# The last three of 96 feed-forward steps cut into halves of 256 columns, where before only the last one was

## The chip, the cores and the metric

The kernel runs on one core of a Trainium2 chip. The metric is the device time of one execution in microseconds (us), as the median of several. Five engines work at once, each through its own queue in the order of that queue: PE (matmuls), ACT (ScalarE), DVE (VectorE), POOL (GpSimd) and SP, which only issues DMAs here. Where one engine needs what another makes, the program has semaphore waits.

## The reference

```python
# attention part: a gated recurrence over 768 time steps, for 4 batches x 8 heads of width 40
attn_out = _attn_ref(q, k, v, i_gate, f_gate, o_gate)
x = attn_out.transpose(0, 2, 1, 3).reshape(3072, 320)
# feed-forward part
h = x @ w_in                                  # (3072, 2048)
h2 = h * h
h3 = h2 * h
P = a[0] + a[1] * h + a[2] * h2 + a[3] * h3
Q = 1.0 + np.abs(b[0]) * np.abs(h) + np.abs(b[1]) * h2
g = P / (Q + 1e-06)
return (g @ w_out).astype(np.float32)         # (3072, 320)
```

The change is in the feed-forward part alone.

## The kernel before, in words

The 3072 tokens go through the feed-forward part in 12 blocks of 256, and each block in 8 steps of 256 of the 2048 hidden features. One step, `feed_forward(n, i)` (line 1098), works on a tile of 128 partitions by 512 columns (`W`, line 1101): columns 0 to 255 (`T` = 256) are the 256 tokens for one group of 128 features, columns 256 to 511 the same tokens for the next group. So the two halves of a step need nothing of each other until their products are added up in `po`. The attention part runs ahead of the feed-forward blocks that need it; in the last block, number 11, no attention work is left.

What one step does, with the names of the planner's operations, the engine, and how a row of the trace shows it:

- `f1` on PE: h = x @ w_in into `ph`, 16 matmuls, 8 for each half. `ph` has one PSUM tile of 128x512 for the whole step (`f_f1`, line 1109), out of a pool of four (`psH`, line 422).
- `ha` (`ha<-ph`), `u` (`w<-ha,ba`) and `p1` (`p<-ph,ps`) on ACT: |h|, a linear form of it, and a shifted square of h.
- `p3` on DVE (`p<-p,ps,ph`): the cubic's next product.
- `w` on POOL (`w<-w,ha`): the denominator Q but for its constant.
- `y` (`ph<-w,cd`) and `r0` (`ph<-ph`) on ACT: 1/Q, by a reciprocal square root and a square, written over h in `ph`.
- `gH` on DVE (`gH<-p,ps,ph`): g in the rounded form that PE takes. Then `m` on DVE (`w<-w,gH`), `rm` on POOL (`p<-p,w`) and `gL` on DVE (`gL<-p,ps,ph`) make the remainder that the rounding left.
- `f2` and `f3` on PE: gH times w_out (8 matmuls) and gL times w_out (4) are added up in `po`, over all 8 steps of a block.
- `ev`: after a block's last step `po` goes to SBUF, in the last block on ACT for its first 128 tokens and on DVE for the others (`ot<-po`), and from there to DRAM by DMA.

A step is written for either form: `cuts` (line 1101) is one slice of 512 columns, or two of 256, and `each` (line 1213) records an operation once for each cut.

```python
last = NS * n + i >= NS * NU // 2 - HALVED                                     # line 1100
cuts = [slice(j * T, (j + 1) * T) for j in range(2)] if last else [slice(0, W)]  # line 1101
...
plan.add(
    f"{name}{'half' if last and part is not None else ''}_{k}", base + FFN_AT[name] + at, engine, cost, fn,
...
for j, c in enumerate(cuts):
    add(
        name, engine, cost * 0.6 if last else cost, lambda c=c: fn(c), r, w,
```

What sets the order: `_Plan` (line 58) gathers all operations with a key and an estimated cost. `order` (line 96) simulates the engines with these costs and gives each engine its queue; of the operations that are about ready it takes the one with the smallest key. The key comes from the table `FFN_AT` (line 173) plus an entry of `NUDGE` (line 196) for this one operation of this one step, if there is one. An operation of a step in halves carries the word "half" in its name, and so has no entry in `NUDGE`. The semaphore waits are put in when the program is built, from the tiles that instructions read and write.

Below, y6.0 is operation y of step 6 of block 11, its first half; y6 is that operation undivided.

Of the kernel before, what the change touches and what calls it, by code (L numbers as in the profile page):

```python
# [190 lines left out]
FIRST = -40  # L191
EARLY = 3
HOT = 90
HALVED = 1

NUDGE = dict(
    raw_j0=20.54, s0_j0=4.61, o0_j0=47.59, raw_i0=-37.31, s0_i0=-2.65, o0_i0=-60.48, o2_i0=-57.94, raw_o0=-4.06,
# [178 lines left out]
def _program(  # L376
# [721 lines left out]
    def feed_forward(n, i):  # L1098
        d = {}
        last = NS * n + i >= NS * NU // 2 - HALVED  # L1100
        cuts = [slice(j * T, (j + 1) * T) for j in range(2)] if last else [slice(0, W)]
# [207 lines left out]
```

## Time and profile before

| | us |
|---|---|
| median of 3 runs | 570.61 (570.03 to 570.77) |
| time of the profiled execution | 571.71 |
| its span, from the first to the last instruction | 569.9 |
| PE busy | 527.2 (93%) |
| DVE busy | 476.2 (84%) |
| ACT busy | 430.9 (76%) |
| POOL busy | 394.5 (69%) |

The rows are of the one profiled execution, which took 1.1 us more than the median; 1.8 us of its time lie outside its span. Times in rows are from the span's start. A row of the order of time gives the start, the length, the engine, the operation with what it writes and reads, how many instructions stand in it, and in brackets the engine's idle time before it with what ended that.

### The profile page before, as it was taken

How to read it: one execution, taken by the hardware profiler on the slowest of the kernel's cores; microseconds unless marked ns; L12 is line 12 of the kernel's file. 1: busy time of each engine (PE TensorE's matmuls, PEld its weight loads, DVE VectorE, ACT ScalarE, POOL GpSimd, SP SyncE). 2: the span in 40 equal slices, each digit the busy share in tenths (PEclk: the TensorE clock that was granted, in tenths of full speed). 3: DMA queues.
4: the chain of work that ended last, by engine and by line, in shares of the span. 5: the costliest groups of instructions: out<-in, count | busy, mean ns of one | idle time of the engine just before them, and what ended most of it. 6: DMA issues, size and time to landing. Idle time of an engine off the chain costs nothing.

```text
span 569.9 us, 13096 instructions
## 1 busy us (share of the span) xinstructions
PE 527.2 (93%) x5024; PEld 493.6 (87%) x5024; DVE 476.2 (84%) x782; ACT 430.9 (76%) x757; POOL 394.5 (69%) x353
## 2 busy tenths in 40 slices
PE   4966896899999999999999999999999999999994
PEld 4964686799989999999999898899899999999993
DVE  8999888997888779988888877877987878878685
ACT  2567679776866888777788868888877777777982
POOL 4538469986677697777868684586777686757753
PEclk9877687999999999999999999999999999999998
DMA  5899966432331213332313214232122010000000
GB/s 171 183 258 243 224 170 139 85 69 56 88 66 55 60 45 81 62 72 78 79 35 85 36 50 97 64 66 74 33 62 73 15 36 2 1 26 1 23 1 30
DMA packets 120666, 44.10 MB, mean 77 GB/s; under 512 B 103826, under 2 KB 113106, under 8 KB 120594
## 3 DMA queue, kind: packets, MB, share of 16 engines
q1 hardware_dynamic: 120450, 43.01, 32.3%
q8 instruction: 41, 0.67, 0.5%
q14 instruction: 31, 0.25, 0.2%
q10 hardware_dynamic: 144, 0.16, 0.1%
HBM read 39.03 MB, written 4.13 MB: 76 GB/s over the span
## 4 chain that ended last, share of the span: by engine, by line
PE 69%; DVE 13%; POOL 5%; issue 4%; ACT 4%; DMA 2%; SPq 2%; DVEq 0%; POOLq 0%; ACTq 0%
PE ph L34 27%; PE po L34 25%; PE y L34 7%; PE ps L34 4%; PE kq L34 3%; PE ow L34 2%; DVE w L34 2%; DVE gH L34 2%; POOL p L34 2%; DVE gL L34 1%; ACT ph L34 1%; PE px L34 1%; DVE early_kT L34 1%; POOL w L34 1%; POOL tm L34 1%
## 5 line engine op out<-in xcount | busy, mean ns | idle before, releaser
L34 POOL TENSOR_TENSOR p<-p,w 128x512 f32<-128x512 f32 (+1 forms) x97 | 128.8, 1328 | 84.8 <-DVE w L34 78.1
L34 PE MATMUL ph<-xk,wi 128*128 128x256 f32 x1152 | 174.7, 287 | 0.9 <-DVE gL L34 0.7
L34 POOL TENSOR_TENSOR w<-w,ha 128x512 f32<-128x512 f32 (+1 forms) x97 | 138.5, 1428 | 36.4 <-ACT w L34 32.5
L34 PEld LDWEIGHTS ph<-xk,wi 128*128 128x128 f32 x1152 | 152.8, 189 | 6.0 <-issue 2.1
L34 PE MATMUL po<-wo,gH 128*128 128x320 f32 x768 | 135.8, 315 | 1.8 <-DVE gH L34 1.8
L34 PEld LDWEIGHTS po<-wo,gH 128*128 128x128 f32 x768 | 114.9, 188 | 4.8 <-DVE gH L34 2.6
L34 DVE SCALAR_TENSOR_TENSOR gH<-p,ps,ph 128x512 fp32r<-128x512 f32 (+1 forms) x97 | 71.6, 738 | 33.9 <-PE po L34 15.2
L34 ACT ACTIVATE ha<-ph 128x512 f32<-128x512 f32 (+1 forms) x97 | 57.4, 592 | 42.6 <-PE ph L34 42.3
L34 DVE SCALAR_TENSOR_TENSOR w<-w,gH 128x512 f32<-128x512 f32 (+1 forms) x97 | 84.3, 871 | 5.7 <-POOL p L34 0.5
L34 ACT ACTIVATE w<-ha,ba 128x512 f32<-128x512 f32 (+1 forms) x97 | 78.7, 811 | 4.8 <-POOL p L34 0.4
L34 ACT ACTIVATE ph<-w,cd 128x512 f32<-128x512 f32 (+1 forms) x97 | 66.2, 683 | 20.3 <-DVE p L34 14.4
L34 PE MATMUL po<-wo,gL 128*128 128x320 f32 x384 | 77.1, 318 | 4.3 <-DVE gL L34 4.1
L34 DVE SCALAR_TENSOR_TENSOR gL<-p,ps,ph 128x512 fp32r<-128x512 f32 (+1 forms) x97 | 71.2, 735 | 10.4 <-POOL p L34 8.8
L34 DVE SCALAR_TENSOR_TENSOR p<-p,ps,ph 128x512 f32<-128x512 f32 (+1 forms) x97 | 71.0, 736 | 4.3 <-ACT p L34 3.4
L34 PEld LDWEIGHTS po<-wo,gL 128*128 128x128 f32 x384 | 59.3, 188 | 8.4 <-DVE gL L34 6.6
L34 ACT ACTIVATE p<-ph,ps 128x512 f32<-128x512 f32 (+1 forms) x97 | 65.5, 675 | 0.9 <-DVE gL L34 0.7
L34 ACT ACTIVATE ph<-ph 128x512 f32<-128x512 f32 (+1 forms) x97 | 56.1, 579 | 2.7
L34 PE MATMUL ph<-xk,wj 128*128 128x256 f32 x192 | 54.3, 283 | 0.0
L34 PE MATMUL ph<-xk,wY 128*128 128x256 f32 x192 | 53.9, 281 | 0.0
L34 DVE TENSOR_TENSOR_SCAN e<-fb,eye 128x512 f32<-128x512 f32 x24 | 37.1, 1544 | 0.2
L34 PE MATMUL ps<-qb,kT 104*64 104x128 f32 x384 | 28.9, 297 | 8.2 <-ACT qb L34 5.5
L34 PEld LDWEIGHTS ph<-xk,wY 128*128 128x128 f32 x192 | 36.4, 190 | 0.0
(127 smaller groups left out, 788.7 us busy)
## 6 DMA issues: line engine op xcount, KB each, us to landing
fb<-scrF SPq DMA_DIRECT2D x48, 128.0 KB, 3.1
ab<-scrA SPq DMA_DIRECT2D x48, 128.0 KB, 3.3
rawo<-in_moe_w_out_dram SPq DMA_DIRECT2D x8, 640.0 KB, 5.9
rawi<-in_moe_w_in_dram SPq DMA_DIRECT2D x8, 512.0 KB, 5.6
og<-in_o_gate_dram SPq DMA_DIRECT2D x24, 160.0 KB, 3.4
kr<-in_k_dram SPq DMA_DIRECT2D x24, 160.0 KB, 2.8
qn<-in_q_dram SPq DMA_DIRECT2D x24, 160.0 KB, 3.4
vb<-in_v_dram SPq DMA_DIRECT2D x48, 80.0 KB, 2.8
```

Of the source, the lines that this page charges most:

```text
L34: made = fn(*args, **kwargs)
```

## The change

`HALVED` (line 194) goes from 1 to 3. So steps 5 and 6 of block 11 are cut as step 7 was already: for each of their eleven operations on ACT, DVE and POOL there are two of 128x256 in place of one of 128x512, 22 instructions more in all. PE has the same matmuls in the same order; half of `f2` and `f3` of these steps can now wait for half of gH and gL.

```diff
-HALVED = 1
+HALVED = 3
```

The names of these operations change, so they lose their entries in `NUDGE`, and their order with it. On ACT before, from step 6's first operation to step 7's (names: ha, w and p are the tiles of u, p1 and so on; the figure behind the name is the step):

```order
L34 ACTIVATE ha_6_7309<-ph_6_7279 128x512 [waits PE_49]
L34 ACTIVATE w_6_7318<-ha_6_7309,ba 128x512 [waits Activation_49,Pool_49]
L34 ACTIVATE p_6_7325<-ph_6_7279,ps 128x512 [waits DVE_49]
L34 ACTIVATE ph_5_7237<-w_5_7289,cd 128x512 [waits DVE_49,Pool_49]
L34 ACTIVATE ph_5_7237<-ph_5_7237 128x512 [waits Activation_49]
L34 ACTIVATE ph_6_7279<-w_6_7318,cd 128x512 [waits DVE_49,Pool_49]
L34 ACTIVATE ph_6_7279<-ph_6_7279 128x512 [waits Activation_49]
L34 ACTIVATE ha_7_7371<-ph_7_7327 128x256 [waits PE_49]
```

The same stretch of ACT after, up to y6.0:

```order
L34 ACTIVATE ha_6_7319<-ph_6_7279 128x256 [waits PE_49]
L34 ACTIVATE w_6_7324<-ha_6_7319,ba 128x256 [waits Activation_49,Pool_49]
L34 ACTIVATE ph_5_7237<-w_5_7288,cd 128x256 [waits DVE_49,Pool_49]
L34 ACTIVATE ph_5_7237<-ph_5_7237 128x256 [waits Activation_49]
L34 ACTIVATE ph_5_7237<-w_5_7288,cd 128x256 [waits Activation_49,Pool_49]
L34 ACTIVATE ph_5_7237<-ph_5_7237 128x256 [waits DVE_49]
L34 ACTIVATE p_6_7361<-ph_6_7279,ps 128x256
L34 ACTIVATE ha_6_7319<-ph_6_7279 128x256
L34 ACTIVATE w_6_7324<-ha_6_7319,ba 128x256 [waits Activation_49]
L34 ACTIVATE p_6_7361<-ph_6_7279,ps 128x256
L34 ACTIVATE ha_7_7385<-ph_7_7329 128x256 [waits PE_49]
L34 ACTIVATE ph_6_7279<-w_6_7324,cd 128x256 [waits DVE_49,Pool_49]
```

Step 6's p1.0, ha.1, u.1 and p1.1 stand behind step 5's y and r0 now, where p1 and all of ha and u stood ahead of them; and r05.1 has a wait on DVE. On DVE before, from p3 of step 6 to gH of step 7:

```order
L34 SCALAR_TENSOR_TENSOR p_6_7325<-p_6_7325,ps,ph_6_7279 128x512 [waits PE_49,Activation_49]
L34 SCALAR_TENSOR_TENSOR gH_5_7355<-p_5_7301,ps,ph_5_7237 128x512 [waits DVE_49,PE_49,Activation_49]
L34 SCALAR_TENSOR_TENSOR w_5_7289<-w_5_7289,gH_5_7355 128x512 [waits DVE_49]
L34 SCALAR_TENSOR_TENSOR gH_6_7373<-p_6_7325,ps,ph_6_7279 128x512 [waits PE_49,Activation_49]
L34 SCALAR_TENSOR_TENSOR w_6_7318<-w_6_7318,gH_6_7373 128x512 [waits DVE_49,Pool_49]
L34 SCALAR_TENSOR_TENSOR gL_5_7388<-p_5_7301,ps,ph_5_7237 128x512 [waits Pool_49]
L34 SCALAR_TENSOR_TENSOR p_7_7382<-p_7_7382,ps,ph_7_7327 128x256 [waits Activation_49]
L34 SCALAR_TENSOR_TENSOR p_7_7382<-p_7_7382,ps,ph_7_7327 128x256
L34 SCALAR_TENSOR_TENSOR gL_6_7405<-p_6_7325,ps,ph_6_7279 128x512 [waits PE_49,Pool_49]
L34 SCALAR_TENSOR_TENSOR gH_7_7411<-p_7_7382,ps,ph_7_7327 128x256 [waits DVE_49,PE_49,Activation_49]
```

The same stretch of DVE after:

```order
L34 SCALAR_TENSOR_TENSOR p_6_7361<-p_6_7361,ps,ph_6_7279 128x256 [waits Activation_49]
L34 SCALAR_TENSOR_TENSOR gL_5_7376<-p_5_7293,ps,ph_5_7237 128x256 [waits Pool_49]
L34 SCALAR_TENSOR_TENSOR p_6_7361<-p_6_7361,ps,ph_6_7279 128x256 [waits Activation_49]
L34 SCALAR_TENSOR_TENSOR gH_6_7401<-p_6_7361,ps,ph_6_7279 128x256 [waits DVE_49,PE_49,Activation_49]
L34 SCALAR_TENSOR_TENSOR w_6_7324<-w_6_7324,gH_6_7401 128x256 [waits DVE_49]
L34 SCALAR_TENSOR_TENSOR gH_6_7401<-p_6_7361,ps,ph_6_7279 128x256 [waits Activation_49]
L34 SCALAR_TENSOR_TENSOR w_6_7324<-w_6_7324,gH_6_7401 128x256 [waits DVE_49,Pool_49]
L34 SCALAR_TENSOR_TENSOR gL_6_7422<-p_6_7361,ps,ph_6_7279 128x256 [waits PE_49,Pool_49]
L34 SCALAR_TENSOR_TENSOR p_7_7413<-p_7_7413,ps,ph_7_7329 128x256 [waits Activation_49] x2
L34 SCALAR_TENSOR_TENSOR gL_6_7422<-p_6_7361,ps,ph_6_7279 128x256 [waits Pool_49]
L34 SCALAR_TENSOR_TENSOR gH_7_7435<-p_7_7413,ps,ph_7_7329 128x256 [waits PE_49,Activation_49]
```

Step 5's gH and m stand ahead of p3 of step 6 now, where p3 of step 6 stood ahead of them; and p3 of step 7 stands behind gH and m of both halves of step 6 and behind gL6.0, each half of it with a wait on ACT.

## Rows read from the trace of the kernel before

**Rows 1.** The page's chain that ended last: share of the span by engine.
```profile
PE 69%; DVE 13%; POOL 5%; issue 4%; ACT 4%; DMA 2%; SPq 2%; DVEq 0%; POOLq 0%; ACTq 0%
```

**Rows 2.** PE in order of time, the last 12 us.
```profile
558.23 0.86 PE L34 MATMUL po<-wo,gL 128*128 128x320 f32 x4 [1.15 <-DVE gL L34]
...
563.85 0.56 PE L34 MATMUL po<-wo,gL 128*128 128x320 f32 x2 [0.37 <-DVE gL L34]
```

**Rows 3.** ACT in order of time, steps 5 to 7 of block 11.
```profile
546.18 0.60 ACT L34 ACTIVATE ha<-ph 128x512 f32<-128x512 f32 x1 [0.67 <-PE ph L34]
...
547.89 0.81 ACT L34 ACTIVATE w<-ha,ba 128x512 f32<-128x512 f32 x1
...
551.37 0.69 ACT L34 ACTIVATE p<-ph,ps 128x512 f32<-128x512 f32 x1
552.08 0.69 ACT L34 ACTIVATE ph<-w,cd 128x512 f32<-128x512 f32 x1
552.81 0.58 ACT L34 ACTIVATE ph<-ph 128x512 f32<-128x512 f32 x1
...
554.79 0.38 ACT L34 ACTIVATE ha<-ph 128x256 f32<-128x256 f32 x1
555.21 0.60 ACT L34 ACTIVATE w<-ha,ba 128x256 f32<-128x256 f32 x1
555.71 0.46 ACT L34 ACTIVATE p<-ph,ps 128x256 f32<-128x256 f32 x1
...
559.05 0.48 ACT L34 ACTIVATE ph<-w,cd 128x256 f32<-128x256 f32 x1 [1.62 <-DVE p L34]
559.57 0.37 ACT L34 ACTIVATE ph<-ph 128x256 f32<-128x256 f32 x1
560.54 0.48 ACT L34 ACTIVATE ph<-w,cd 128x256 f32<-128x256 f32 x1 [0.61 <-DVE gH L34]
561.05 0.37 ACT L34 ACTIVATE ph<-ph 128x256 f32<-128x256 f32 x1
```

**Rows 4.** DVE in order of time, the same stretch and the end.
```profile
548.87 1.80 DVE L34 SCALAR_TENSOR_TENSOR w<-w,gH 128x512 f32<-128x512 f32 x1
...
551.26 0.73 DVE L34 SCALAR_TENSOR_TENSOR p<-p,ps,ph 128x512 f32<-128x512 f32 x1
...
558.10 0.86 DVE L34 SCALAR_TENSOR_TENSOR p<-p,ps,ph 128x256 f32<-128x256 f32 x2
...
559.97 0.48 DVE L34 SCALAR_TENSOR_TENSOR gH<-p,ps,ph 128x256 fp32r<-128x256 f32 x1 [0.31 <-ACT ph L34]
560.48 0.42 DVE L34 SCALAR_TENSOR_TENSOR w<-w,gH 128x256 f32<-128x256 f32 x1
...
564.46 0.55 DVE L34 TENSOR_SCALAR ot<-po,pa 128x320 f32<-128x320 f32 x1 [0.66 <-PE po L34]
```

**Rows 5.** POOL in order of time, the same stretch.
```profile
548.84 1.29 POOL L34 TENSOR_TENSOR w<-w,ha 128x512 f32<-128x512 f32 x1 [0.45 <-ACT w L34]
...
556.24 0.74 POOL L34 TENSOR_TENSOR w<-w,ha 128x256 f32<-128x256 f32 x1
...
560.99 0.73 POOL L34 TENSOR_TENSOR p<-p,w 128x256 f32<-128x256 f32 x1 [1.41 <-DVE w L34]
```

**Rows 6.** Stretches: us; busy time and count of PE, PEld, DVE, ACT, POOL; PE clock; DMA.
```profile
80.00:90.00 10.00, 8.20 (x98) 6.97 (x96) 8.65 (x16) 8.91 (x17) 8.16 (x7) 1.00 0.78 202
90.50:97.00 6.50, 5.01 (x68) 4.65 (x70) 5.54 (x9) 6.45 (x10) 6.50 (x6) 0.50 0.78 168
...
561.40:564.50 3.10, 2.02 (x9) 1.19 (x8) 1.82 (x5) 0.22 (x2) 1.04 (x2) 1.00 0.01 3
564.50:569.90 5.40, 0.00 (x0) 0.00 (x0) 0.51 (x1) 0.33 (x1) 0.00 (x0) 0.53 0.26 79
```

**Rows 7.** PE groups by shape, one kind of matmul from 90.5 to 97, then from 80 to 90.
```profile
L34 PE MATMUL ow<-vb,pm 128*40 128x82 f32 x16 | 1.3, 344 | 0.8 <-issue 0.8
...
L34 PE MATMUL ow<-vb,pm 128*40 128x82 f32 x16 | 0.8, 238 | 0.0
```

## The prediction

> **What bounds the kernel now.** I read the chain that ended last first: 69% of it is PE [rows 1]. With a bound of that kind, work on ACT, DVE and POOL is free as long as PE finds something to do. But the change sits in the last three steps, where PE has nothing left to put in between, so I then read each engine's own rows there. PE waits: 1.15 us for gL5, and its last two matmuls stand behind 0.37 us of waiting for gL7.1 [rows 2]. ACT tells why: y7.0 starts at 559.05 after 1.62 us of idleness, released by p3 of step 7 on DVE [rows 3]. From there one piece of work follows the other: y, r0, gH, m, rm, gL, the last two matmuls, and ot, which ends at 564.46 + 0.55 = 565.01 [rows 4]. So the end hangs on when y7.0 starts, and on what stands between it and ot.
>
> The row that decides most here is y7.1 at 560.54 [rows 3]. It works on the second half of `ph`; gH7.0, which ends at 559.97 + 0.48 = 560.45 [rows 4], reads the first. No data goes from one to the other, yet ACT stood idle for 0.61 us and the profile puts that down to gH. The two halves lie in one `ph` tile, and the program lets ACT and DVE at that tile in turn only, whichever half they want.
>
> **Prices.** In halves ha takes 0.38, u 0.60, p1 0.46, y 0.48 and r0 0.37, against 0.60, 0.81, 0.69, 0.69 and 0.58 whole [rows 3]; so a half costs clearly more than half. On DVE half a gH takes 0.48 and half an m 0.42; two halves of p3 take 0.86 together, and I count 0.48 for one, as for gH [rows 4]. POOL takes 0.74 and 0.73 for halves of w and rm, 1.29 for a whole w [rows 5]. Handing over costs 0.03 from ACT to DVE (r0 ends at 559.94, gH starts at 559.97), 0.09 from DVE to ACT (560.45 to 560.54) and 0.04 from one ACT instruction to the next that needs it (554.79 + 0.38 to 555.21); an ACT instruction that needs nothing starts 0.10 before the end of the one ahead (555.21 + 0.60 to 555.71) [rows 3, 4].
>
> **The change part by part.** All times are of the profiled execution, up to y5 at 552.08 and from there on.
>
> 1. *A gain ahead of y5.* ha5.0 is 0.22 shorter than ha5, so y4, r04 and u5.0 stand 0.22 earlier on ACT; u5.0 starts at 547.67, ends at 548.27, and POOL follows 0.14 later (as 548.70 to 548.84 before) at 548.41, until 549.15. m4 on DVE is what this helps: it reads only SBUF, and took 1.80 before because POOL's w5 had started 0.03 ahead of it; it ended 0.54 after w5 did [rows 4, 5]. Now it ends at 549.15 + 0.54 = 549.69, in place of 550.67: 0.98 earlier. Behind it stand gL3 and p3 of step 5, which in halves takes 0.86 for 0.73. y5.0 starts 0.85 earlier: **-0.85**.
> 2. *Step 5's y and r0.* The waits in the order of after resolve to y5.0, r05.0, y5.1, then gH5.0 on DVE, then r05.1. That is 0.48 + 0.04 + 0.37 + 0.04 + 0.48 + 0.03 + 0.48 + 0.09 + 0.37 = 2.38. Step 7 in the trace of before took 561.05 + 0.37 - 559.05 = 2.37 for the same; a whole step takes 1.31 (552.08 to 553.39) [rows 3].
> 3. *Step 6's rest of the front.* p1.0, ha.1, u.1 and p1.1 of step 6 were done ahead of y5 before, while ACT waited anyway. Now they are queued behind r05.1: 0.36 + 0.28 + 0.64 + 0.36 = 1.64.
> 4. *p3 6.0* now waits for p1 6.1, the last reader of `ph` on ACT, and y6.0 for p3 6.0: 0.03 + 0.48 + 0.09 = 0.60.
> 5. *Step 6's y and r0:* 2.38, and p3 6.1 stands between y6.0 and r06.0, each waiting for the other's engine: 0.03 + 0.48 + 0.09 in place of 0.04, so 2.94.
> 6. *Step 7's front* (ha7.0 fits under item 4): u.0, p1.0, ha.1, u.1, p1.1 take 0.50 + 0.36 + 0.28 + 0.64 + 0.36 = 2.14. p1 7.1 also waits for p3 7.0, which DVE reaches only behind gL6.0 and so behind rm6.0 and m6.1: from the start of gH6.0 ACT would be ready after 2.14, DVE is done with p3 7.0 after about 2.36 and hands over. That is 0.30 more, and 0.09 to y7.0.
>
> From y5.0 to y7.0 this makes 2.38 + 1.64 + 0.60 + 2.94 + 2.14 + 0.30 + 0.09 = 10.09. Before it was 559.05 - 552.08 = 6.97: **+3.12**.
>
> 7. *From y7.0 to the end* it was 565.01 - 559.05 = 5.96. Now p3 7.1 stands between y7.0 and r07.0 as in item 5; gL6.1, which DVE does ahead of gH7.0, ends before r07.0 and costs nothing: **+0.56**.
>
> Nothing else moves. PE's order is the same; its work behind the last f1 is four steps of 12 matmuls, and it is done with all that it can have long before the last gL. No transfer changes but the last two, which start when ot ends. POOL's w halves are each done before the y that needs them; what covers them is the very chain above, so they would show only if that chain were shorter.
>
> **Sum:** -0.85 + 3.12 + 0.56 = +2.83. On the profiled execution's 571.71 that gives 574.5, with a span of 572.7. The median is 1.1 below that execution, and the change is in a stretch that every run has, so I add the same to it: 570.61 + 2.8 = **573.4**.
>
> Bounds: item 6's 0.30 may vanish if DVE is a little ahead, and m4 may gain some 0.2 more, so +2.3 at least. At most, an m of step 5, 6 or 7 meets a POOL operation once more; a half on POOL is 0.74, so I allow +0.4: +3.2. The clock comes on top (below). Three runs before lay 0.7 apart, so I add 0.3 at either side.
>
> Item 6 is where a rule weighs something that no row isolates: p1 7.1 and p3 7.0 both only read `ph`, and other halves of it. By the rows I might let them run side by side, since the only wait that a row shows is of a write (y) for a read. The Trainium skill, "PSUM — Partial Sum Buffer", section "PSUM bank collisions raise a hardware error", says that two engines may not be in one bank at the same partitions at once, reads against reads included, and that semaphores should guard a bank and not an address; a 128x512 tile of 4 bytes fills such a bank. By that page halves of one tile are no separate resources, and item 6 keeps its 0.30; without it the sum would be +2.5.
>
> **Rivals.** *The halves run past each other* (570.61 - 0.9 = 569.7). This is what a reader of the diff would expect: no data links them. Then items 2 and 5 lose the steps on DVE (2.38 becomes 0.48 + 0.04 + 0.37 - 0.10 + 0.48 + 0.04 + 0.37 = 1.68; 2.94 becomes 1.68), item 4 hides behind ACT's own queue, and y5.0 to y7.0 takes 1.68 + 1.64 - 0.10 + 0.28 + 1.68 - 0.10 + 2.14 + 0.09 = 7.3, or +0.3. The -0.85 stays, and y7.1 no longer waits for gH7.0, which gives back some 0.4 at the end. It decides from where the handing over between ACT and DVE inside a step costs less than about a quarter of the 3.7 us that it makes of the difference to my sum. Against it stand the 0.61 before y7.1 and DVE named as the wait of r05.1 in the order of after. Chance 0.09.
>
> *The clock falls in the tail* (574.0). PE's granted clock was 1.00 up to 564.5, with PE busy for 2.02 of the last 3.10 us, and 0.53 in the stretch behind it, where PE did nothing [rows 6]. After the change PE has the same last matmuls spread over about 3 us more, and some may run at the lower of the two levels, 1.2 GHz. The nearest rows at either level are 344 and 238 ns for one kind of matmul in stretches at 0.50 and 1.00 [rows 6, 7]. The last eight matmuls, 0.1 longer each, make 0.85; part of it falls into waits, at the least only the last one counts. I take 0.6: +3.4. Chance 0.17.
>
> *Only part of the chain holds* (571.4). ACT's items 2 to 6 could be shorter if DVE, ahead by the 0.98 that m4 gained, took step 6's p3 early; but p3 6.0 waits for p1 6.1. Chance 0.06.
>
> **How the numbers follow.** My forecast has 0.68: it lies from 570.61 + 2.3 - 0.3 to 570.61 + 3.2 + 0.3, so 572.6 to 574.1. With the clock's case the range is 572.6 to 574.5, and holds about 0.83. Some 0.2%, or 1.1 us, is what a measurement of this kernel can tell from no change. Of the first rival I give 0.04 to faster and 0.05 to no change, of the third 0.04 to no change and 0.02 to slower; all else is slower: 0.04, 0.09, 0.87.
>
> **What would show it.** Right: ACT rows of step 6 with idle time before r0 and y, released by DVE; y7.0 about 2.3 us later than 559.05; m4 shortened from 1.80 to about 0.8 to 1.0; PE waiting for gH6.0 (it was ready when PE came to it before); the last ot ending near 567.8. Wrong: y5.1 or y6.1 starting while DVE is still at the other half; y7.0 at or before 559; ACT's wait of 0.61 before the second y gone. If the end is later than 568.3, I look at the PE clock in the last 5 us and at m beside POOL.

## The result, and the profile after

| | before | after |
|---|---|---|
| median, us | 570.59 (568.44 to 571.94) | 573.05 (571.56 to 574.82) |
| ratio to before, with its 95% interval | | 1.0047 (1.0029 to 1.0065) |
| profiled execution, us | 571.71 | 573.43 |
| its span, us | 569.9 | 571.6 |

The change makes the kernel slower, by 0.3 to 0.65%. The median is 0.35 below the forecast of 573.4, inside the range of 572.6 to 574.5.

The two profiled executions differ already where the program doesn't: ha of step 5 starts at 546.18 before [rows 3] and at 545.08 after, 1.10 earlier. So I compare from a point that both share, the first f1 matmul of step 6, which is 1.10 earlier too. The stretch from there to the end of the last `ot` is called the **tail** below. PE at that point, in order of time, first of before:

```profile
547.75 0.87 PE L34 MATMUL ph<-xk,wi 128*128 128x256 f32 x6
```

and of after, with the end of the program:

```profile
546.65 0.87 PE L34 MATMUL ph<-xk,wi 128*128 128x256 f32 x6
...
557.29 1.78 PE L34 MATMUL po<-wo,gH 128*128 128x320 f32 x8 [1.38 <-DVE gH L34]
...
561.61 0.57 PE L34 MATMUL po<-wo,gL 128*128 128x320 f32 x2 [1.81 <-DVE gL L34]
...
563.63 1.06 PE L34 MATMUL po<-wo,gH 128*128 128x320 f32 x4 [0.62 <-DVE gH L34]
564.55 1.84 PE L34 MATMUL po<-wo,gL 128*128 128x320 f32 x4
```

The tail is 565.01 - 547.75 = 17.26 before [rows 4] and 566.98 - 546.65 = 20.33 after (566.43 + 0.55 below). That is **+3.07**, or 0.54% of the time. PE waits 1.38 for gH6.0 now, for which it didn't wait before, and longer for step 6's gL (1.81 for gL6.1) and for gH7.1. The last two matmuls, which wait for gL7.1, are slower too: PE ends 0.95 behind gL7.1 (564.96 + 0.48 = 565.44 to 566.39), where it was 0.61 before (563.32 + 0.48 = 563.80 to 564.41 [rows 2]).

ACT of after, in order of time: step 5's first ha, and everything that matters here from step 5's y on:

```profile
545.08 0.38 ACT L34 ACTIVATE ha<-ph 128x256 f32<-128x256 f32 x1 [0.67 <-PE ph L34]
...
550.13 0.48 ACT L34 ACTIVATE ph<-w,cd 128x256 f32<-128x256 f32 x1 [0.30 <-DVE p L34]
550.64 0.37 ACT L34 ACTIVATE ph<-ph 128x256 f32<-128x256 f32 x1
551.11 0.48 ACT L34 ACTIVATE ph<-w,cd 128x256 f32<-128x256 f32 x1
552.13 0.37 ACT L34 ACTIVATE ph<-ph 128x256 f32<-128x256 f32 x1 [0.55 <-DVE gH L34]
...
554.76 0.48 ACT L34 ACTIVATE ph<-w,cd 128x256 f32<-128x256 f32 x1 [0.33 <-DVE p L34]
555.78 0.37 ACT L34 ACTIVATE ph<-ph 128x256 f32<-128x256 f32 x1 [0.55 <-DVE p L34]
556.25 0.48 ACT L34 ACTIVATE ph<-w,cd 128x256 f32<-128x256 f32 x1
557.27 0.37 ACT L34 ACTIVATE ph<-ph 128x256 f32<-128x256 f32 x1 [0.55 <-DVE gH L34]
...
559.61 0.48 ACT L34 ACTIVATE p<-ph,ps 128x256 f32<-128x256 f32 x1 [0.19 <-DVE p L34]
560.18 0.48 ACT L34 ACTIVATE ph<-w,cd 128x256 f32<-128x256 f32 x1
561.20 0.37 ACT L34 ACTIVATE ph<-ph 128x256 f32<-128x256 f32 x1 [0.55 <-DVE p L34]
562.18 0.48 ACT L34 ACTIVATE ph<-w,cd 128x256 f32<-128x256 f32 x1 [0.61 <-DVE gH L34]
```

DVE of after, the same stretch:

```profile
547.55 1.04 DVE L34 SCALAR_TENSOR_TENSOR w<-w,gH 128x512 f32<-128x512 f32 x1
...
551.62 0.48 DVE L34 SCALAR_TENSOR_TENSOR gH<-p,ps,ph 128x256 fp32r<-128x256 f32 x1 [0.86 <-ACT ph L34]
...
555.27 0.48 DVE L34 SCALAR_TENSOR_TENSOR p<-p,ps,ph 128x256 f32<-128x256 f32 x1 [0.22 <-ACT ph L34]
...
556.75 0.48 DVE L34 SCALAR_TENSOR_TENSOR gH<-p,ps,ph 128x256 fp32r<-128x256 f32 x1 [1.00 <-ACT ph L34]
...
566.43 0.55 DVE L34 TENSOR_SCALAR ot<-po,pa 128x320 f32<-128x320 f32 x1 [0.99 <-PE po L34]
```

ACT and DVE take turns. r05.1 waits 0.55 for gH5.0, which works on the other half; r06.0 waits 0.55 for p3 6.1, again the other half; r06.1 waits 0.55 for gH6.0. Before, only step 7 had such a wait on ACT, the 0.61 ahead of y7.1 [rows 3]. PE's clock in three stretches of after; columns as in [rows 6], the clock is the number after POOL's:

```profile
557.50:561.40 3.90, 2.07 (x10) 1.28 (x9) 2.67 (x7) 3.04 (x8) 2.97 (x4) 1.00 0.00 0
561.40:564.50 3.10, 2.26 (x10) 1.54 (x10) 2.36 (x6) 1.01 (x3) 1.04 (x2) 0.94 0.00 0
564.50:567.00 2.50, 1.86 (x5) 1.00 (x4) 1.03 (x2) 0.53 (x1) 0.42 (x1) 0.50 0.04 10
```

0.94 over 3.10 us is what 1.00 makes with 0.50 for the last 0.37: the clock went to the lower level (1.2 GHz) at about 564.1, with the last matmuls still to come. Before, it was 1.00 until they were done [rows 6].

**A correction.** The description of the kernel ahead of the prediction says that a halved operation loses its entry in `NUDGE` and its order with it. That is wrong here: `NUDGE` has entries for feed-forward operations of blocks 0 to 3 alone, so those of block 11 have none to lose. By the code, the order changes because the planner takes the halves as tiles of their own, each at 0.6 of the cost and each with the urgent key of its y and r0; so a first half's y and r0 are ready earlier and go ahead of the next step's front. It doesn't know that the program will make two halves of one tile wait for each other. The sum rested on the order as printed and on rows, not on that sentence.

### The profile page after: what moved, and what is told of

Same layout as the page of the kernel before. It is cut to its first block, busy times and chain, and to the rows that moved or that the text cites. A ratio compares the mean times of both kernels' runs of the same rounds, so it can differ in the third digit from the quotient of the medians.

```text
span 571.6 us, 13121 instructions
## 1 busy us (share of the span) xinstructions
PE 525.0 (92%) x5024; PEld 490.6 (86%) x5024; DVE 476.2 (83%) x790; ACT 432.8 (76%) x767; POOL 395.4 (69%) x357
## 4 chain that ended last, share of the span: by engine, by line
PE 68%; DVE 12%; POOL 6%; ACT 4%; issue 4%; SPq 3%; DMA 2%; DVEq 0%; POOLq 0%; ACTq 0%
PE ph L34 27%; PE po L34 25%; PE y L34 6%; PE ps L34 4%; PE ow L34 3%; PE kq L34 3%; DVE w L34 2%; ACT ph L34 2%; DVE gH L34 2%; PE px L34 1%; DVE gL L34 1%; DMA rawj<-in_moe_w_in_dram 1%; POOL p L34 1%; DVE early_kT L34 1%; POOL w L34 1%
## 5 line engine op out<-in xcount | busy, mean ns | idle before, releaser
L34 PEld LDWEIGHTS ph<-xk,wj 128*128 128x128 f32 x192 | 36.3, 189 | 0.0
```

The costliest lines, as they stand in the source:

```text
L34: made = fn(*args, **kwargs)
```

## The experiments

Three theories were to be told apart. **Turns**: the halves of a step lie in one `ph` tile, and ACT and DVE get at it in turn only. **Pieces**: more and shorter instructions cost more by themselves. **Order**: step 6's and 7's fronts now stand behind the y and r0 of the step ahead. What came out, with the tail in us and y7.0 counted from the same first f1 matmul:

| kernel | steps in halves | `ph` of the halves | tail | y7.0 at | ratio to before (95%) |
|---|---|---|---|---|---|
| before | 7 | one tile | 17.26 | 11.31 | |
| after | 5, 6, 7 | one tile | 20.33 | 13.53 | 1.0047 (1.0029 to 1.0065) |
| e1_banks | 5, 6, 7 | two tiles | 16.21 | 10.64 | 0.9968 (0.9947 to 0.9990) |
| e8_own_tiles_again | 5, 6, 7 | two tiles | 16.22 | 10.68 | 0.9982 (0.9967 to 0.9997) |
| e2_pair | 7 (5, 6 in pairs) | one tile | 17.84 | 11.89 | 1.0013 (0.9992 to 1.0034) |
| e3_late_y | 5, 6, 7, y late | one tile | 18.01 | 10.76 | 1.0026 (1.0006 to 1.0045) |
| e10_own_tiles_late_y | 5, 6, 7, y late | two tiles | 17.87 | 9.56 | one execution |
| e4_warm | 5, 6, 7 | one tile | 20.00 | as after | one execution |
| e5_own_tile_step7 | 7 | two tiles | 16.38 | 10.91 | 0.9997 (0.9981 to 1.0013) |
| e6_two_steps | 6, 7 | one tile | 19.97 | 11.48 | 1.0051 (1.0032 to 1.0071) |
| e9_own_tiles_two_steps | 6, 7 | two tiles | 17.84 | 10.63 | one execution |
| e7_no_step | none | one tile | 17.42 | 10.65 (whole) | 1.0011 (0.9997 to 1.0026) |

Each tail comes from one profiled execution. It is still the finer measure: executions of one kernel lie some 3 to 5 us apart, mostly through what happens earlier. The two profiled executions of the kernel with own tiles have spans of 565.8 and 569.2, and tails of 16.21 and 16.22.

**Own tiles for the halves.** The changed kernel, but the second half of `ph` of steps 5, 6 and 7 in a PSUM tile of its own, in slots that are free by then:

```diff
+        def second(i):
+            pool, tag = {5: (psA, "a"), 6: (psT, "tu"), 7: (psH, "h")}[i]
+            return pool.tile([P, W], F32, tag=tag, name=f"pb{n}_{i}")
+        def hh(c):
+            return d["hb"][:, 0:T] if last and c.start else d["h"][:, c]
...
-            nc.scalar.activation(tl("ha")[:, c], d["h"][:, c], AF.Abs)
+            nc.scalar.activation(tl("ha")[:, c], hh(c), AF.Abs)
```

and so for every reader and writer of `ph`. ACT, DVE and POOL keep the changed kernel's order.

> The changed kernel with one thing different: the second half of ph of steps 5, 6 and 7 lies in a PSUM tile of its own (two in the tiles that the attention part has left, step 7's in a fourth ph slot). ACT, DVE and POOL have the same instructions in the same order; on PE one f2 of step 4 stands ahead of step 7's second f1 half. Measured from step 6's first f1 matmul to the end of the last ot: 17.26 us before, 20.33 after the change. Theory A (the halves of one tile take turns between ACT and DVE): the waits across halves are gone, so 16.2 to 16.6, about 1 us less than the kernel before, some 569.5 to 569.9 in the median, ratio to before 0.998; no idle time on ACT released by gH of the other half. Theory B (the price is that of 22 more and shorter instructions and of their order): 20.0 to 20.4 as after the change, 573.0, ratio 1.0045.

ACT of this kernel, step 5's first ha, and step 7's y and r0 (the second halves are called `pb`):

```profile
542.49 0.38 ACT L34 ACTIVATE ha<-ph 128x256 f32<-128x256 f32 x1
...
555.45 0.47 ACT L34 ACTIVATE ph<-w,cd 128x256 f32<-128x256 f32 x1
555.95 0.37 ACT L34 ACTIVATE ph<-ph 128x256 f32<-128x256 f32 x1
556.55 0.48 ACT L34 ACTIVATE pb<-w,cd 128x256 f32<-128x256 f32 x1 [0.24 <-POOL w L34]
557.06 0.37 ACT L34 ACTIVATE pb<-pb 128x256 f32<-128x256 f32 x1
```

and DVE beside it:

```profile
556.37 0.47 DVE L34 SCALAR_TENSOR_TENSOR gH<-p,ps,ph 128x256 fp32r<-128x256 f32 x1
...
557.47 0.48 DVE L34 SCALAR_TENSOR_TENSOR gH<-p,ps,pb 128x256 fp32r<-128x256 f32 x1 [0.16 <-ACT pb L34]
```

y7.1 runs from 556.55 while gH7.0 is under way until 556.84; it waited for its own input, POOL's w, and no longer for gH. r07.1 follows y7.1 after 0.03. The tail is 16.21: 4.12 shorter than after's, and 1.05 shorter than before's. So the shared tile sets the whole loss. The gain over the kernel before is for the most part step 7's: with an own tile there and steps 5 and 6 whole, the tail is 16.38 (below), so cutting these two steps is worth some 0.17.

The shared tile made ACT wait for PE as well. After the change ha5.0 reads the first half of `ph` and yet starts only when PE is done with the second (the 0.67 in the row at 545.08), 1.57 ahead of step 6's first f1 matmul; with own tiles it starts at 542.49, 2.32 ahead of that matmul (544.81).

The Trainium skill, "PSUM — Partial Sum Buffer", section "PSUM bank collisions raise a hardware error", asks for a guard by bank and not by address; this program's waits for `ph` go by the whole tile, which gives the same: with one tile ACT stood still for the other half's reader, with two it didn't. Tiles in SBUF are another matter. Step 7's tile `w` was one tile in every run, and in the kernel before ACT's u7.1 wrote its second half from 556.47 to 557.07, while POOL's w7.0 wrote its first from 556.24 to 556.98 [rows 5], and neither waited for the other:

```profile
556.47 0.60 ACT L34 ACTIVATE w<-ha,ba 128x256 f32<-128x256 f32 x1
```

Whether the chip would stand two engines in one PSUM tile is nothing that a run here tried.

The gain over the kernel before was near what its interval could show, so the same kernel ran again:

> The kernel with three steps in halves and own PSUM tiles for the second halves, once more: its first comparison gave 0.9968 with an interval from 0.9947 to 0.999, while the last step alone with an own tile, whose tail is longer by only 0.17, gave 0.9997. If the gain of 1.05 us in the tail is all there is, the time is 0.8 to 1.3 us under the kernel before, a ratio of 0.9977 to 0.9986, and the tail is 16.1 to 16.4 again. If the first comparison was a matter of chance as a whole, the tail is 17 or more and the ratio 1.000.

The tail is 16.22, and the ratio 0.9982, with an interval wholly below 1 (569.27 against 570.16). The first ratio, 0.9968, was more than the tail explains; the second is what 1.05 of 570 makes.

**The pieces alone.** The kernel before in its own order, each operation of ACT, DVE and POOL in steps 5 and 6 issued as two halves one right behind the other:

```diff
+        pair = not last and NS * n + i >= NS * NU // 2 - 3
...
-                    name, engine, cost * 0.6 if last else cost, lambda c=c: fn(c), r, w,
+                    name, engine, cost * 0.6 if last else cost, (lambda: [fn(slice(0, T)), fn(slice(T, W))]) if pair else lambda c=c: fn(c), r, w,
```

> The kernel before, with each ACT, DVE and POOL operation of steps 5 and 6 issued as two instructions of 256 columns right behind each other, in the place of the one of 512: as many instructions as after the change, in the order of before, on one ph tile. From step 6's first f1 matmul to the end of ot: 17.26 before, 20.33 after. Theory A (turns between ACT and DVE inside a step, which this order avoids, since both halves of an operation run on one engine in a row): 17.7 to 18.1, some 0.6 us more than before, 571.1, ratio 1.001. Theory B (number and length of the instructions): near 20, 573, ratio 1.0045.

ACT, step 5's y and r0:

```profile
552.25 1.06 ACT L34 ACTIVATE ph<-w,cd 128x256 f32<-128x256 f32 x2
553.34 0.77 ACT L34 ACTIVATE ph<-ph 128x256 f32<-128x256 f32 x2
```

Two halves back to back take 1.06 for y, against 0.69 whole, and 0.77 for r0, against 0.58 [rows 3], and the tail grows by 0.58. That is as many instructions as after has, at a fifth of its loss: the pieces are not what makes it.

**The order alone.** The changed kernel, with y of steps 5 and 6 so much less urgent that the next step's front goes ahead again:

```diff
-    plan.nudge = NUDGE
+    plan.nudge = dict(NUDGE, **{'yhalf_11_5': 400.0, 'yhalf_11_6': 400.0}) if square else NUDGE
```

> The changed kernel, with y of steps 5 and 6 given a later place by their keys, so that ACT does the next step's ha, u and p1 ahead of them as far as they are ready. One ph tile for a step as after the change. From step 6's first f1 matmul to the end of ot: 20.33 after the change. Theory C (step 6's front behind step 5's y, items 3 and 6 of the sum, is a price of its own): 18.5 to 19.2, so 1.2 to 1.8 less than after the change, 571.6 to 572.0, ratio 1.002. If only the turns inside a step count (items 2, 4, 5, 7): 20.0 or more, 573.0.

The tail is 18.01, below the 18.5 to 19.2 that I expected, and 1.99 less than after's without its clock (20.00, below). So with one tile the order decides 1.99 of the 2.74 that are lost without the clock. The fourth corner of the square is the same late y with own tiles:

> The fourth corner of a square: three steps in halves, second halves of ph in tiles of their own, and y of steps 5 and 6 late, so that the next step's front goes ahead of it as in the run with one tile for both halves (tail 18.01 there; 20.33 with the order of the changed kernel, 0.33 of that by the clock; 16.21 and 16.22 with own tiles and the order of the changed kernel). If turns and order each have a price that adds up, the late y would take some 2.0 off once more, and the tail could not be over 16 (it would be near 14.5, which the last step's own chain hardly allows: from y7.0 to the end alone it is 5.5). If the order costs only through the turns, the late y gains nothing here: 16.2 or more. Worked out from the durations of the rows and the waits of the program I expect 16.9 to 17.3, since gH5 and gH6, and PE's f2 behind them, come later than with own tiles alone.

PE of that kernel, in order of time, and two stretches of it:

```profile
559.63 0.96 PE L34 MATMUL po<-wo,gL 128*128 128x320 f32 x4 [2.08 <-DVE gL L34]
560.42 2.17 PE L34 MATMUL po<-wo,gH 128*128 128x320 f32 x8
562.39 1.27 PE L34 MATMUL po<-wo,gL 128*128 128x320 f32 x4
```

```profile
559.00:562.00 3.00, 2.37 (x11) 2.28 (x12) 1.75 (x5) 0.00 (x0) 0.72 (x1) 0.77 0.01 3
562.00:565.00 3.00, 1.66 (x7) 1.26 (x5) 0.55 (x1) 0.53 (x1) 0.00 (x0) 0.66 0.07 24
```

The last 16 matmuls ran one behind the other from 559.63 to 563.66, 4.03, much of it at the lower clock. The late y with one tile has the same sequence at full clock:

```profile
563.53 0.95 PE L34 MATMUL po<-wo,gL 128*128 128x320 f32 x4 [2.65 <-DVE gL L34]
564.32 1.34 PE L34 MATMUL po<-wo,gH 128*128 128x320 f32 x8
565.49 0.75 PE L34 MATMUL po<-wo,gL 128*128 128x320 f32 x4
```

That is 2.71, so I estimate that the clock took 1.32 of the 17.87, and that without it the tail would be 16.55. My 16.9 to 17.3 holds neither figure. The question it was run for is answered either way: the late y gains 1.99 with one tile and nothing with two (16.55 or more against 16.21). With three steps in halves, by these single executions, the order costs only through the turns.

**How the loss grows with the steps.** `HALVED` = 2:

> HALVED = 2: steps 6 and 7 in halves, step 5 whole. If the turns of the halves and the order set the loss, step 5's own share goes (the two turns of y5, r05 and gH5, 2.4 less the two whole operations it replaces, some 0.5 to 0.9, and the gain of 0.85 ahead of y5 too), and step 6's stays: y and r0 of step 6 take turns with p3 6.1 and gH6.0 between them, and p3 of step 7 stands behind them. The tail, from step 6's first f1 matmul to the end of the last ot, is then 19.5 to 20.1 (17.26 before, 20.33 with three steps cut, of it 0.33 by the clock): nearly all of the loss with one step cut. If the loss were in proportion to the steps cut (a price for each halved instruction, 11 of 22 here), it would be 18.6 to 19.0.

ACT of it, y6.1 and y7.1:

```profile
554.53 0.48 ACT L34 ACTIVATE ph<-w,cd 128x256 f32<-128x256 f32 x1 [1.21 <-DVE p L34]
...
560.01 0.48 ACT L34 ACTIVATE ph<-w,cd 128x256 f32<-128x256 f32 x1 [2.41 <-DVE gL L34]
```

The tail of 19.97 is as expected, nearly the whole loss with one more step cut; the places are not. Step 6's y and r0 don't alternate with DVE as I had said; ACT stands idle for 1.21 ahead of y6.1, and for 2.41 ahead of y7.1. DVE in between:

```profile
557.64 0.48 DVE L34 SCALAR_TENSOR_TENSOR gH<-p,ps,ph 128x256 fp32r<-128x256 f32 x1 [0.87 <-ACT p L34]
...
558.97 0.47 DVE L34 SCALAR_TENSOR_TENSOR p<-p,ps,ph 128x256 f32<-128x256 f32 x1
559.50 0.48 DVE L34 SCALAR_TENSOR_TENSOR gL<-p,ps,ph 128x256 fp32r<-128x256 f32 x1
```

gH7.0 waits 0.87 for p1 7.1, which only reads the other half of `ph`. (Both use step 7's SBUF tile `p` too, but that isn't it: with own tiles p1 7.1 runs from 557.66 to 558.13, and gH7.0 beside it from 557.78.) y7.1 then needs p3 7.1, which is queued behind gH7.0, m7.0 and gL6.1 and ends at 559.44. Yet y7.1 starts only at 560.01, behind gL7.0 (559.50 + 0.48 = 559.98), which reads the first half: one more turn. Here PE's clock fell too: from gH7.1's f2 to the end it takes 564.73 - 561.46 = 3.27, and 564.07 - 561.13 = 2.94 in the next kernel, 0.33 more. That next kernel is the same with own tiles:

> HALVED = 2 with the second halves of steps 6 and 7 in PSUM tiles of their own: with one tile for both halves the tail was 19.97, of it about half a microsecond by the clock. If the turns in one tile are what makes that loss, own tiles take most of it away, 1.5 to 2.2 of it: 17.8 to 18.4. What then still lies above the kernel before (17.26) is the order: y6.0 and r06.0 stand right behind r05 and ahead of the rest of step 6's front and of step 7's, so y6.1 and y7.1 start late all the same. If there is no price of the order once the turns are gone, it is 16.2 to 16.6, as with one or three steps and own tiles.

The tail is 17.84: own tiles take 1.80 of the loss away without the clock's share, and 0.58 above the kernel before is left. ACT shows where:

```profile
559.68 0.48 ACT L34 ACTIVATE pb<-w,cd 128x256 f32<-128x256 f32 x1 [1.55 <-POOL p L34]
```

and DVE just before:

```profile
559.11 0.48 DVE L34 SCALAR_TENSOR_TENSOR p<-p,ps,pb 128x256 f32<-128x256 f32 x1
```

ACT still stands idle for 1.55 ahead of y7.1. The row names POOL, where rm7.0 ended at 558.88 + 0.73 = 559.61; but rm7.0 writes `p`, which y7.1 doesn't touch. What y7.1 has to wait for is p3 7.1, which reads the h that y7.1 writes over. It ends at 559.59, 0.09 ahead of y7.1, as DVE has it queued behind gH7.0, m7.0 and gL6.1. gL7.0, behind which y7.1 stood with one tile, runs beside it now, from 559.64. So here the order has a price without turns. That it had none with three steps holds for that order and no other.

**The last step alone.** First with its second half in an own tile, then not cut at all:

> The kernel before, with the last step alone in halves as it has been, and that step's second half of ph in a PSUM tile of its own. This tells which of the two things in the run with three steps in halves and own tiles brought its gain: the tile, or the cutting of steps 5 and 6. Measured from step 6's first f1 matmul to the end of the last ot (17.26 before, 16.21 with three steps cut and own tiles). If it is the tile, step 7's own y, r0 and gH no longer take turns and the tail is 16.4 to 16.7, the time some 0.6 to 0.9 under the kernel before; steps 5 and 6 in halves are then worth 0.2 to 0.4 more at the best. If it is the cutting, step 7's own tile is worth the one wait of r07.1 for gH7.0 less r0 in between, 0.1 to 0.3, and the tail is 17.0 to 17.2. Both theories leave everything ahead of step 7's y as it was: y7.0 within 0.1 of its 11.31 from the anchor.

ACT of it, y and r0 of both halves of step 7:

```profile
559.12 0.48 ACT L34 ACTIVATE ph<-w,cd 128x256 f32<-128x256 f32 x1 [1.22 <-DVE p L34]
559.64 0.37 ACT L34 ACTIVATE ph<-ph 128x256 f32<-128x256 f32 x1
560.07 0.48 ACT L34 ACTIVATE pb<-w,cd 128x256 f32<-128x256 f32 x1
560.58 0.37 ACT L34 ACTIVATE pb<-pb 128x256 f32<-128x256 f32 x1
```

The tail is 16.38, by the tile alone; three steps in halves with own tiles had 16.21. Of the 0.88 gained, 0.48 lie between y7.0 and the end (the 0.61 ahead of y7.1 [rows 3] is gone), and 0.40 ahead of y7.0, which I had said would stay: y7.0 needn't wait for p3 7.1 any more, only for p3 7.0. The time doesn't confirm the gain: 0.9997, with an interval that holds both 0.9985, which is what 0.88 makes, and no change.

> HALVED = 0: no step in halves, the last one whole too. If halves of one PSUM tile that take turns gain as little for step 7 as they lost for steps 5 and 6, the tail from step 6's first f1 matmul to the end of the last ot is 17.3 to 17.7 against 17.26 before, so that cutting step 7 alone was worth 0 to 0.4. If cutting a step whose halves no next step has to pass is worth what it is meant to (gH of the second half beside f2 of the first, and gL so too), the tail is 18.2 to 19.2.

The tail is 17.42, or 0.16 more than with step 7 cut: in one tile, cutting the last step had been worth next to nothing.

**The clock.** The changed kernel, with 17 more matmuls of 128 columns, whose result nobody reads, put into PE's waits (6 ahead of the f2 of gH6.0, 8 ahead of the f3 of gL6.1, 3 ahead of the f2 of gH7.1):

```diff
+            many = {(6, 0, False): 6, (6, 1, True): 8, (7, 1, False): 3}.get((i, j, low), 0) if n == NU // 2 - 1 else 0
...
+                for _ in range(many):
+                    nc.tensor.matmul(idle["t"][:, 0:P], ident, ident, start=True, stop=True)
```

> The changed kernel with 17 matmuls of 128 columns more on PE, which nobody reads, put into its waits ahead of gH6.0 (6), gL6.1 (8) and gH7.1 (3). It asks whether the last matmuls pay for a clock that fell in the tail (granted 0.94 from 561.4 to 564.5 and 0.50 behind that in the changed kernel; the last pair of matmuls took 0.63 for its last instruction against 0.42 in the kernel before). If PE's idleness is what lowers it: granted clock 1.00 up to the last matmul, last f3 matmul 0.42, and from step 6's first f1 matmul to the end of ot 20.0, 0.3 less than 20.33. If not: 0.50 and 0.63 as before, 20.3 to 20.5.

```profile
561.40:564.50 3.10, 3.07 (x21) 2.49 (x20) 2.36 (x7) 1.21 (x3) 0.73 (x1) 1.00 0.00 0
564.50:567.00 2.50, 1.51 (x7) 0.71 (x5) 1.39 (x4) 0.53 (x1) 0.73 (x1) 1.00 0.04 10
```

The clock, in the same stretches as above, stays at 1.00 and the tail is 20.00, 0.33 less than after's. So of the +3.07 some 0.33 is the clock, and 2.74 the chain.

## Why the prediction was right, point by point

Steps as numbered in the prediction, in us; the measured values are differences of starts in the ACT and DVE rows of after, with durations of the last one added where an end is meant.

| step | forecast | measured |
|---|---|---|
| 1, ha of step 5 to y5.0, against before | -0.85 | 550.13 - 545.08 = 5.05 against 552.08 - 546.18 = 5.90: -0.85 |
| 2, y5.0 to the end of r05.1 | 2.38 | 552.13 + 0.37 - 550.13 = 2.37 |
| 3 and 4, to y6.0 | 2.24 | 554.76 - 552.50 = 2.26 |
| 5, y6.0 to the end of r06.1 | 2.94 | 557.27 + 0.37 - 554.76 = 2.88 |
| 6, to y7.0 | 2.53 | 560.18 - 557.64 = 2.54 |
| y5.0 to y7.0, against 6.97 | 10.09 | 10.05 |
| 7, y7.0 to the end, against 5.96 | +0.56 | 566.98 - 560.18 = 6.80: +0.84, of it 0.33 the clock |
| sum | +2.83 | +3.07, without the clock +2.74 |

- *Step 1.* m4 took 1.04, as it ends 0.54 after POOL's w half (547.31 + 0.74), just as 1.80 did before. With own tiles m4 started at 545.38, 0.04 ahead of POOL's w, and took 0.69, and POOL's half took 1.26 for 0.74. The Trainium skill, "SBUF — State Buffer", section "Who interferes with whom", says that an operation of VectorE with two inputs in SBUF contends with one of GpSimd that reads SBUF, for ports that are an exclusive lock, and that the order of issue decides which of the two is held up; the three pairs agree.
- *Item 6* kept 0.30 for reads of different halves. p1 7.1 did wait for p3 7.0 (0.19 in the row at 559.61, where both only read `ph`), and the sum to y7.0 came out at 2.54 for 2.53. The 0.87 ahead of gH7.0 in the kernel with two steps says it again.
- *Item 7* was short by 0.28: the clock's 0.33, less 0.05 that the chain itself was shorter. The clock I had as a case of its own at +0.6. That case came true in the profiled execution, at about half its price: PE had to wait around the earlier of its last matmuls anyway, so only the two that stand behind the last gL count.
- *The rival of the halves that run past each other* was put at 0.9 below the kernel before, and own tiles give 1.05 in the tail. That the two lie so close is in part luck, as its terms come out otherwise. From step 6's first f1 matmul to y5.0 it takes 2.69 for 4.33, or 1.64 less where the rival counts 0.85, with ha5.0, which no longer waits for PE's second half, 0.75 earlier; y5.0 to y7.0 takes 7.95 where it counts 7.3, with 0.30 of waiting for POOL's w ahead of y5.1. The 0.4 at the end came as counted (5.56 for 5.96). In the changed kernel the rival fell for the one reason named, the shared tile.
- *The rival of the part of the chain* had no room: p3 6.0 started at 554.18, right behind p1 6.1, which ended at 554.15.
- *What the prediction missed* is that its list of costs holds two causes that need each other: items 3, 4 and 6, the fronts that stand late, cost only because the halves take turns. It priced them as a sum and came out right, since both are present. A reader who had taken item 3's 1.64 as the price of the order for itself would have gone wrong: with two tiles that order is the best of those tried.

## What to carry to other kernels

Cutting work into halves to hand it over sooner pays only if the halves are separate wherever the program's waits look. Here that was the PSUM tile, and not the tiles in SBUF: cut the PSUM tile with the work, or the engines take turns and the finer steps cost more than the coarse ones (20.33 against 17.26; with own tiles 16.21). Then ask how many steps need the cut: the last one alone, with its own tile, brought 0.88 of the 1.05. Where a wait in the trace is put down to an engine that works on other data, look what they share before cutting further. And a planner that takes the pieces as free of each other, as this one did, may put them in an order in which each turn costs more.

## What the runs showed of the hardware that I had not expected

PE's clock fell in some tails and not in others, and no single number in the rows says which. It was at 0.50 for the last matmuls of the changed kernel, whose longest wait was 1.81, and of the kernel with two steps and one tile, whose longest was 1.45 (0.33 each), and for most of the last 16 with own tiles and late y, after a wait of 2.08, where it cost some 1.32. It stayed at 1.00 through a wait of 2.00 in the kernel with pairs, and through one of 2.65 with one tile and late y. Each is one execution. That filling the waits holds the clock at 1.00 was seen once and paid 0.33; what decides when it falls stays open.
